# A retention and feed-forward kernel on one core: blocks of 256 tokens, nine equal tiles, 64-key chunks on quarters of the array

## The chip, the cores and the metric

The kernel runs on one core of one Trainium2 chip. The metric is device time in microseconds of one execution, and lower is better. One execution was also recorded by the hardware profiler; its times are counted from the first instruction of the program.

## What is computed

The reference joins two stages. The first is a retention layer on q, k and v, each of shape (8 batches, 8 heads, 576 positions, 64), the second a feed-forward layer with the activation h * cos(h) on 4608 tokens of width 512 and an inner width of 2048.

```python
scores = (q @ k^T) / sqrt(64)
gamma = 1 - 2 ** (-5 - head)
ret = scores * where(i >= j, gamma ** (i - j), 0)     # per head, i query, j key position
x = (ret @ v), heads side by side: (4608, 512)
h = x @ w_in                                           # (4608, 2048)
out = (h * cos(h)) @ w_out                             # (4608, 512)
```

Inputs and output are float32; the matmuls run in bfloat16.

## The kernel before

The decay factors as gamma ** i times gamma ** -j, so queries and keys are scaled by position tables first (`gq`, `gk`). Retention then needs no decay in the mask: within a group of tokens it is scores, a causal mask and a product with v; what came earlier enters through a running sum of k-times-v products per head, called the state. The positions are counted from the middle of a sequence, MID = 288.

Tokens are cut into 36 groups of 128. Sequences have 576 positions, so two sequences are nine groups, and in the group with index MIX = 4 of the nine the first half ends one sequence and the second half begins the next. For each group `load` fetches q, k and v with rows of 256 bytes, `prep` scales q and k on GpSimd into `qks` and rounds v to `vb`, and `transposes` makes `qkT`, on TensorE for the first six groups and by a transposing DMA afterwards. `scores` multiplies keys and queries into PSUM, and VectorE applies the mask into `ret`. `state` (for early groups) and `states` (for pairs of groups) form the k-times-v sums, `attn_out` adds the group's own product (`own`) and the product with the state (`carried`), and ScalarE copies the result to `xT`. Four groups at the very start share one load of q with 1024-byte rows (`fq4`).

The feed-forward part goes by tiles of tokens with widths 512, 256, 256 and seven times 512. `mm1` makes eight blocks of h per tile; for each, ScalarE takes the cosine into `cosh` and VectorE multiplies into `gT`. The blocks take turns on three PSUM areas, "a", "b" and "m". The second matmul has two forms. The first three tiles use `mm2`, sixteen products per 128 tokens. From the fourth tile on (S7 = 3), `mm2_seven` computes the 2x2 block product with seven products instead of eight, each of 16 matmuls of 256 columns, in the order 1, 2, 6, 4, 7, 5, 3. This needs sums of quarters of gT (`g_sum`, numbers 3, 5 and 6 on VectorE, number 7 on GpSimd) and of w_out (`w_sums`). PSUM areas "n" and "st" take the products' results.

The order of work on every engine is the order in which the Python code emits it (`manual_schedule`). Retention for later tiles is interleaved by hand: in the first three tiles through a list `todo` of positions in mm2's stream, later through the dictionary `at`, which calls `unit7` before product 2, 5, 6 or 3. `feed` paces loads, preparations and transposes by the stores of the output. Additions left over are kept in a list `pend` and emitted by `flush` at the next product.

Of the kernel before, what the change touches and what calls it, by code (L numbers as in the profile page):

```python
# [17 lines left out]
def kernel(  # L18
# [9 lines left out]

# [4 lines left out]
    HG = H // 2  # L39
    DM, DF = moe_w_in.shape  # L40
# [3 lines left out]
    NG = NTOK // P  # L44
    PER = 2 * S // P
    MIX = PER // 2
    HP = P // 2
# [3 lines left out]
    ET = DF // P  # L51

    widths = [512, 256, 256] + [512] * 7
    assert sum(widths) == NTOK
    starts = [sum(widths[:n]) for n in range(len(widths))]
    N_PE_T = 6
    S7 = 3
    LD = 5

    consts = ctx.enter_context(tc.tile_pool(name="consts", bufs=1))  # L60
    first = ctx.enter_context(tc.tile_pool(name="first", bufs=1))
    ld = ctx.enter_context(tc.tile_pool(name="ld", bufs=LD))
    nat = ctx.enter_context(tc.tile_pool(name="nat", bufs=8))
    trp = ctx.enter_context(tc.tile_pool(name="trp", bufs=8))
    retp = ctx.enter_context(tc.tile_pool(name="retp", bufs=4))
# [4 lines left out]
    op = ctx.enter_context(tc.tile_pool(name="op", bufs=2))  # L70
    xp = ctx.enter_context(tc.tile_pool(name="xp", bufs=2))

# [4 lines left out]

    pos_i = consts.tile([P, PER, H], I32)
    pos = consts.tile([P, PER, H], F32)
    lng = consts.tile([P, H], F32)  # L80
    gq = consts.tile([P, PER, H], F32)
    pos_i4 = consts.tile([P, 4, H], I32)
    pos4 = consts.tile([P, 4, H], F32)
    gq4 = consts.tile([P, 4, H], F32)
    gk = consts.tile([P, PER, H], F32)
    ln_scale = consts.tile([P, 1], F32)
    half_pi = consts.tile([P, 1], F32)
    tri = consts.tile([P, P], F32)
    tri_mix = consts.tile([P, P], F32)
    diag2 = consts.tile([P, P], F32)  # L90
    ident = consts.tile([P, P], BF16)
    zeros = consts.tile([P, 512], BF16)
    w_in_sb = consts.tile([P, DG, DF], BF16)
    w_out_sb = consts.tile([P, ET, DM], BF16)

    v_odd = consts.tile([P, 2, H, D], BF16)

    blocks4 = [consts.tile([P, HG, D], BF16, tag=f"sb{x}", name=f"sb{x}") for x in range(4)]

    tiles = {}  # L100
# [4 lines left out]
    def load(g, names="qkv", gate=None):  # L105

        t0 = g * P
        if g % PER == MIX:
            parts = [(0, HP, t0), (HP, P, t0 + HP)]
        else:  # L110
            parts = [(0, P, t0)]
        for name in names:
            src = {"q": q, "k": k, "v": v}[name]
            f = ld.tile([P, H, D], F32, tag="f" + name, name=f"f{name}")
            for p0, p1, t in parts:
                b, s0 = divmod(t, S)
                i = nc.sync.dma_start(
                    f[p0:p1], src[b, :, s0 : s0 + p1 - p0, :].rearrange("h s d -> s h d")
                )
                if gate is not None:  # L120
                    tc.add_manual_dep(
                        i.ins, gate.ins.name,
                        mybir.DependencyInfo(
                            mybir.DependencyClass.Sync, mybir.DependencyReason.DATA
                        ),
                        reason="weights first",
                    )
                    gate = None
            tiles["f" + name, g] = f

    def prep(g, early=False, kv_first=False):

        c = g % PER
        fk, fv = (tiles.pop(("f" + n, g)) for n in "kv")
        qks = nat.tile([P, 2, H, D], BF16, tag="qks", name="qks")
        vb = nat.tile([P, H, D], BF16, tag="vb", name="vb")
        qkT = trp.tile([P, 2 * HG, P], BF16, tag="qkT", name="qkT")

        def scaled(eng, m, f, by):
            eng.tensor_tensor(  # L140
                out=qks[:, m].rearrange("p (b a) d -> p a b d", a=2),
                in0=f.rearrange("p (a b) d -> p a b d", a=2),
                in1=by[:, c, :].rearrange("p (a b) -> p a b", a=2).unsqueeze(3).to_broadcast(
                    [P, 2, HG, D]
                ),
                op=ALU.mult,
            )

        if not early and not kv_first:
            scaled(nc.gpsimd, 0, tiles.pop(("fq", g)), gq)  # L150
        scaled(nc.vector if g == 3 else nc.gpsimd, 1, fk, gk)
        if early:
            tiles["fv", g] = fv
        else:
            nc.gpsimd.tensor_copy(vb, fv)  # L155
            if c == MIX and g > PER:
                nc.gpsimd.tensor_copy(v_odd[HP:, g // PER % 2], fv[HP:])
        if kv_first:
            scaled(nc.gpsimd, 0, tiles.pop(("fq", g)), gq)
        qT = qT4[:, :, g * P : (g + 1) * P] if early else qkT[:, :HG, :]  # L160
        tiles["a", g] = (qks, vb, qkT, qT)

    def transposes(g, banks=None, only=(0, 1)):
        qks, vb, qkT, qT = tiles["a", g]
        if g >= N_PE_T:
            nc.sync.dma_start(qkT, qks.rearrange("s m h d -> s (m h d)"), transpose=True)
            return
        for m in only:
            ps = psum.tile([P, HG, P], BF16, tag=banks[m], name="tr")
            for hg in range(HG):  # L170
                nc.tensor.transpose(
                    ps[:, hg, :],
                    qks[:, m, 2 * hg : 2 * hg + 2, :].rearrange("s h d -> s (h d)"),
                    ident,
                )
            nc.scalar.copy(qkT[:, m * HG : (m + 1) * HG, :], ps)
        if ("fv", g) in tiles and g != 3:
            nc.scalar.copy(vb, tiles.pop(("fv", g)))

    def warm(ps, n):  # L180


        for _ in range(n):
            nc.tensor.matmul(ps, lhsT=zeros[:, :P], rhs=zeros, start=True, stop=True)

    def scores(g, bank, idle=0, parts=1, put_off=None):
        qks, vb, qkT, qT = tiles["a", g]
        ps = psum.tile([P, 2, HG, P], F32, tag=bank, name="sc")
        warm(ps[:, 0].rearrange("p b i -> p (b i)"), idle)
        for hg in range(HG):  # L190
            for i0 in range(0, P, P // parts):
                for he in range(2):
                    d0, i1 = he * D, i0 + P // parts
                    nc.tensor.matmul(  # L194
                        ps[i0:i1, he, hg, :],
                        lhsT=qkT[d0 : d0 + D, HG + hg, i0:i1],
                        rhs=qT[d0 : d0 + D, hg, :],
                        start=True,
                        stop=True,
                    )  # L200
        ret = retp.tile([P, 2, HG, P], BF16, tag="ret", name="ret")
        mask = tri_mix if g % PER == MIX else tri
        tiles["ret", g] = ret

        def masked():
            nc.vector.tensor_tensor(  # L206
                out=ret.rearrange("p a b i -> p (a b) i"),
# [5 lines left out]
        if put_off is None:  # L213
            masked()
        else:
            put_off.append(masked)
# [502 lines left out]
    for g in (4, 5):  # L719
        prep(g)  # L720
# [148 lines left out]
```

## Time and profile before

| what | value |
|---|---|
| median of 3 runs | 301.75 us (301.12 to 301.95) |
| the profiled execution | 301.3 us |
| its span, first to last instruction | 299.6 us |
| TensorE busy | 286.9 us (96%) |
| VectorE busy | 215.1 us (72%) |
| ScalarE busy | 134.1 us (45%) |
| GpSimd busy | 138.9 us (46%) |
| granted TensorE clock, mean | 0.991 |
| DMA | 50.29 MB in 154305 packets |

Busy times are those of the profile's engine rows: PE is TensorE's matmuls, PEld its weight loads, DVE VectorE, ACT ScalarE, POOL GpSimd, SP the engine that issues most DMAs. Matmuls are pipelined, so their mean length holds some 0.2 us of latency; the distance between starts is what a matmul costs in a stream. A line such as `<-DVE gs L437` names what ended a wait: the VectorE instruction of line 437 that writes gs.

### The profile page before, as it was taken

The numbers are of one execution on the slowest core, as the hardware profiler recorded it, in microseconds if no ns is written. First come the engines' busy times: TensorE is split into PE (matmuls) and PEld (weight loads), VectorE is DVE, ScalarE is ACT, GpSimd is POOL, SyncE is SP. The second block draws the span as 40 slices with busy tenths as digits, with TensorE's granted clock in tenths as the row PEclk, the third lists the DMA queues.
The fourth block names the chain that finished last, engine by engine and source line by source line (L and its number), as shares of the span: only waits on it lengthen the run. The fifth ranks groups of instructions, "written<-read, shape, count | busy, mean of one in ns | idle before, by whom it ended". The sixth has DMA issues, their size and how long they took to land.

```text
span 299.6 us, 7314 instructions
## 1 busy us (share of the span) xinstructions
PE 286.9 (96%) x3105; PEld 196.5 (66%) x3105; DVE 215.1 (72%) x262; ACT 134.1 (45%) x163; POOL 138.9 (46%) x151
## 2 busy tenths in 40 slices
PE   7899999999999878999999999999999999999994
PEld 3478647848478757547854785488548854884584
DVE  6776717664568986599678966896689669925943
ACT  3556333515245314553355542644364445525620
POOL 2750067436345797473863791379238113101410
PEclk9999999999999979999999999999999999999998
DMA  8999999999999999997999999996960250011013
GB/s 210 214 210 207 209 217 194 218 210 237 202 170 227 209 242 222 201 233 165 213 216 247 199 218 206 194 234 160 209 117 3 79 135 0 31 51 63 0 37 106
DMA packets 154305, 50.29 MB, mean 168 GB/s; under 512 B 140832, under 2 KB 153248, under 8 KB 154272
## 3 DMA queue, kind: packets, MB, share of 16 engines
q1 hardware_dynamic: 149504, 45.10, 78.9%
q0 software_dynamic: 4224, 4.19, 8.4%
q8 instruction: 24, 0.39, 0.6%
q10 hardware_dynamic: 544, 0.52, 0.5%
q14 instruction: 9, 0.07, 0.1%
HBM read 36.70 MB, written 9.44 MB: 154 GB/s over the span
## 4 chain that ended last, share of the span: by engine, by line
PE 54%; DVE 5%; ACT 1%; issue 0%; DVEq 0%
PE h L364 25%; PE o L497 24%; DVE gT L373 2%; PE ov L332 1%; PE sc L194 1%; PE st L265 1%; PE ov L318 1%; DVE gs L437 1%; DVE ot L517 1%; DVE ret L206 1%; ACT cosh L372 0%; DVE s L286 0%; ACT ot L521 0%; DVEq L864 0%; DVEq L517 0%
## 5 line engine op out<-in xcount | busy, mean ns | idle before, releaser
L364 PE MATMUL h<-xT,w_in_sb 128*128 128x512 bf16 (+2 forms) x832 | 127.6, 314 | 0.8 <-DVE xT L349 0.7
L373 DVE TENSOR_TENSOR gT<-h,cosh 128x1024 bf16<-128x1024 f32 x72 | 88.0, 1223 | 37.3 <-ACT cosh L372 37.2
L372 ACT ACTIVATE cosh<-h,half_pi 128x1024 f32<-128x1024 f32 x72 | 80.2, 1114 | 66.7 <-PE h L364 66.0
L364 PEld LDWEIGHTS <-w_in_sb 128*128 128x128 bf16 x832 | 75.7, 98 | 50.0 <-issue 1.3
L437 POOL TENSOR_TENSOR gs<-gT 128x512 bf16<-128x512 bf16 x28 | 36.0, 1293 | 78.7 <-DVE gT L373 78.7
L140 POOL TENSOR_TENSOR qks<-fq,gq 128x512 bf16<-128x512 f32 x32 | 35.0, 1092 | 48.8 <-DMA fq<-in_q_dram 48.6
L497 PEld LDWEIGHTS <-gs 128*128 128x128 bf16 x456 | 44.0, 99 | 9.4 <-DVE gs L437 3.1
L140 POOL TENSOR_TENSOR qks<-fk,gk 128x512 bf16<-128x512 f32 x35 | 38.6, 1104 | 9.7 <-DMA fk<-in_k_dram 9.1
L206 DVE TENSOR_TENSOR ret<-sc,tri 128x1024 bf16<-128x1024 f32 x32 | 38.1, 1218 | 2.7 <-PE sc L194 2.7
L521 ACT COPY ot<-o 128x512 f32<-128x512 f32 x28 | 16.4, 586 | 45.7 <-PE o L497 44.6
L497 PEld LDWEIGHTS <-gT 128*128 128x128 bf16 x336 | 32.5, 98 | 6.0 <-DVE gT L373 0.6
L497 PE MATMUL o<-ws,gs 128*128 128x256 bf16 x224 | 28.4, 283 | 2.9 <-DVE gs L437 2.9
L517 DVE TENSOR_TENSOR ot<-ot,o 128x512 f32<-128x512 f32 x34 | 22.6, 682 | 11.0 <-ACT ot L521 7.9
L381 PE MATMUL o<-w_out_sb,gT 128*128 128x512 bf16 x128 | 30.1, 380 | 0.0
L497 PE MATMUL o<-w_out_sb,gs 128*128 128x256 bf16 (+1 forms) x232 | 26.8, 269 | 0.0
L497 PE MATMUL o<-w_out_sb,gT 128*128 128x256 bf16 x224 | 26.5, 273 | 0.3 <-DVE gT L373 0.3
L155 POOL CAST vb<-fv 128x512 bf16<-128x512 f32 x32 | 20.9, 652 | 8.3 <-DMA fv<-in_v_dram 7.7
L349 ACT CAST xT<-ov 128x1024 bf16<-128x1024 f32 (+1 forms) x18 | 16.5, 917 | 14.7 <-PE ov L318 12.6
L381 PEld LDWEIGHTS <-gT 128*128 128x128 bf16 x128 | 11.8, 98 | 12.5
L437 DVE TENSOR_TENSOR gs<-gT 128x512 bf16<-128x512 bf16 (+1 forms) x20 | 13.4, 672 | 0.3
L497 PE MATMUL o<-ws,gT 128*128 128x256 bf16 x112 | 13.4, 272 | 0.0
L391 ACT COPY ot<-o 128x512 f32<-128x512 f32 x8 | 4.7, 588 | 17.8 <-PE o L381 17.8
(69 smaller groups left out, 178.9 us busy)
## 6 DMA issues: line engine op xcount, KB each, us to landing
out_dram<-ot SPq DMA_DIRECT2D x35, 256.0 KB, 3.7
fk<-in_k_dram SPq DMA_DIRECT2D x32, 256.0 KB, 4.9
fv<-in_v_dram SPq DMA_DIRECT2D x32, 256.0 KB, 5.2
fq<-in_q_dram SPq DMA_DIRECT2D x30, 256.0 KB, 4.7
w_in_sb<-in_moe_w_in_dram POOLq DMA_DIRECT2D x4, 512.0 KB, 9.1
w_out_sb<-in_moe_w_out_dram POOLq DMA_DIRECT2D x4, 512.0 KB, 16.3
fq<-in_q_dram SPq DMA_DIRECT2D x8, 128.0 KB, 3.7
fk<-in_k_dram SPq DMA_DIRECT2D x8, 128.0 KB, 4.4
```

The lines of the kernel that those rows point to most:

```text
L140: eng.tensor_tensor(out=qks[:, m].rearrange("p (b a) d -> p a b d", a=2), in0=f.rearrange("p (a b) d -> p a b d", a=2), in1=by[:, c, :].re ...
L155: nc.gpsimd.tensor_copy(vb, fv)
L206: nc.vector.tensor_tensor(out=ret.rearrange("p a b i -> p (a b) i"), in0=ps.rearrange("p a b i -> p (a b) i"), in1=mask.unsqueeze(1).to_br ...
L349: evac(tiles["x", n][:, :, t0 : t0 + len(gs) * P], ps.rearrange("p c x i -> p c (x i)"))
L364: nc.tensor.matmul(ps[:, j, :], lhsT=w_in_sb[:, dg, (et + j) * P : (et + j + 1) * P], rhs=xT[:, dg, c0 : c0 + w], start=(dg == 0), stop=(d ...
L372: nc.scalar.activation(cosh, ps, ACTF.Sin, bias=half_pi, scale=1.0)
L373: nc.vector.tensor_mul(gT[:, et : et + m, c0 : c0 + w], ps, cosh)
L381: nc.tensor.matmul(ps, lhsT=gT[:, et, tsi * P : (tsi + 1) * P], rhs=w_out_sb[:, et, :], start=(et == 0), stop=(et == ET - 1),)
L437: eng.tensor_tensor(out=tiles["gs", n, x][:, e : e + step], in0=a[:, e : e + step], in1=b[:, e : e + step], op=op_,)
L497: nc.tensor.matmul(dst[i], lhsT=lhs[:, e, j * P : (j + 1) * P], rhs=rhs[:, e, c0:c1], start=(fresh and e == 0 and (i == 0 or len(parts) > 2)),
L517: return lambda: nc.vector.tensor_tensor(out=out_, in0=in0, in1=in1, op=ALU.add)
L521: nc.scalar.copy(t, tiles["all", x])
```

## The change

The kernel is written anew around the same two layers. Tokens are cut into 18 blocks of 256, two for each of nine tiles of 512. Tile 0 uses the plain second matmul, tiles 1 to 8 the seven products.

Queries of all blocks, and keys and values of the first six, are loaded with two neighbouring tokens in a partition (rows of 512 bytes); keys and values of later blocks keep one token a partition. Sub-block y of a block holds the even or odd tokens (or the first or second 128). A block's keys form chunks: two of 128 keys in blocks 0 to 5 (`pair`), four of 64 keys in blocks 6 to 17. Every chunk lies on one half of the partitions (x), so that with two heads (he) or two column halves four products of 64 rows and 64 columns lie on quarters of the array. Scores and carried products write PSUM in token order, that is with a stride of two. In `out_own` a drain of TensorE stands between the halves of the work. State sums are kept per chunk.

Blocks 0 to 3 are transposed on TensorE, later ones by DMA. Block 0 and 1 are worked through before mm1 starts, block 2 within tile 0's second matmul, block 3 in the middle of tile 1's mm1, and later ones between the seven products. Sum 7 is made on VectorE in tiles 1 and 2.

The core of the diff:

```diff
-    widths = [512, 256, 256] + [512] * 7
-    N_PE_T = 6
-    S7 = 3
-    LD = 5
+    W = 512
+    NT = NTOK // W
+    BK = 256
+    NB = NTOK // BK
+    NP_B = 6
+    AHEAD = 3
...
+    def scores(j, banks, idle=0):
...
+        for hg in range(HG):
+            for y in range(2):
+                for he in range(2):
+                    for x in range(2):
+                        c = cs[x] if pair else cs[2 * y + x]
+                        nc.tensor.matmul(
+                            in_order(pss[he][c.rows, hg, y, :]),
+                            lhsT=kT[he * D : he * D + D, 1, y, hg, c.rows],
+                            rhs=q_cols(c, he, hg),
+                            start=True,
+                            stop=True,
+                        )
...
+    def out_own(j, ps):
...
+        for swap in (1, 0):
+            for hg in range(0, HG, 2):
+                for c in cs:
+                    he = c.x ^ swap
+                    for y in c.subs:
+                        for h in (head(he, hg), head(he, hg + 1)):
+                            nc.tensor.matmul(
+                                ps[h % 2 * D : h % 2 * D + D, h // 2, c.c0 : c.c0 + c.n],
+                                lhsT=vb[c.rows, y, h, :],
+                                rhs=ret[c.rows, h // HG, h % HG, y, :],
...
+            if swap:
+                nc.tensor.drain()
...
-        eng, step = (nc.gpsimd, 2) if x == 7 else (nc.vector, e1 - e0)
+        eng, step = (nc.gpsimd, 2) if x == 7 and n > 2 else (nc.vector, e1 - e0)
...
+        if n == 1:
+            slots = {0: "w04", 1: "w48", 5: ((7, 0, E2),), 6: ((5, 0, 4),)}
...
             if x == 6:
-                late_sums(n, (3,))
+                late_sums(n, (3, 7) if n < 3 else (3,))
...
+    load(0, "kqv")
+    load(1, "kqv")
...
+    round_v(0)
+    more_tables()
+    scaled(nc.gpsimd, 1, "k", 0)
+    scaled(nc.gpsimd, 1, "k", 1)
+    w_dma = [load_w_in(e, e + 512) for e in range(0, DF, 512)]
+    m0 = scores(0, "ab", idle=2)
+    m0[0]()
+    transpose_pe(1, "k", 0, "n", act)
+    add0 = sums_of(0, "st")
+    m0[1]()
+    add0()(act)
+    scaled(nc.gpsimd, 1, "q", 0)
+    scaled(nc.vector, 1, "q", 1)
+    more_tables2()
+    out_own(0, ps0)
+    out_carried(0, ps0)
...
+    transpose_pe(1, "q", 0, "n", act)
+    transpose_pe(1, "q", 1, "st", act)
+    m1 = scores(1, "ab", idle=2)
+    m1[0]()
+    round_v(1)
+    add1 = sums_of(1, "st")
+    m1[1]()
+    add1()(act)
+    w_dma += [load_w_out(e, e + 4) for e in range(0, ET, 4)]
+    load_next(names="kq", gate=w_dma[5])
...
+    def intro(j, sc_banks, st_bank, put_off=None):
+        ms = scores(j, sc_banks)
+        add = sums_of(j, st_bank)
+        run = [*ms, lambda: add()()]
+        if put_off is None:
+            for f in run:
+                f()
+        else:
+            run[0]()
+            put_off += run[1:]
...
+            if n == 0 and i == 0:
+                inside = {2: lambda: outputs(1, "m", act, vec)}
...
+                if i == 3:
+                    early(3, "q")
+                    steps_to(5)
+                if i == 4:
+                    intro(3, "ab", "st")
+                    outputs(3, "m", act, vec)
+            mm1(n, et, c0, cw, {0: "abmabmab", 1: "abmmabma"}.get(n, "abmabmab")[i], inside)
...
+            todo += [(34, lambda: intro(2, "ab", "b")), (52, lambda: outputs(2, "a", act, vec))]
...
+        def only_intro(flush, pend):
+            flush()
+            intro(a, sc_banks(a), "m" if a < NP_B else "b", pend)
+
+        def mid_unit(flush, pend):
+            flush()
+            outputs(a, "m")
+            intro(b, sc_banks(b), "st" if b < NP_B else "b", pend)
...
+        if n in (1, 2):
+            at = {6: only_intro, 5: mid_unit, 3: end_unit}
+        elif n < last:
+            at = {2: first_unit, 5: second_unit}
```

`sums_of` makes the chunks' k-times-v products into one PSUM area and returns the addition to the running state, one addition for both chunks in blocks 0 to 5 and one for each chunk later. `outputs` calls `out_own`, `out_carried` and the copy to `xT`. `early` prepares or transposes blocks 2 and 3; `steps_to` prepares later blocks on GpSimd, two tiles ahead. `first_unit` and `second_unit` call `outputs` for a block and `intro` for the next; in tile n, a is block 2n + 2 and b is block 2n + 3. In the preamble, `more_tables` holds nine iotas and the masks on GpSimd, `more_tables2` the position tables on VectorE and ScalarE.

## The prediction

> **What bounds the kernel now.** I read the page, then windows cut at the tiles of 512 rows, then the timeline around the one early hole, then single groups for durations.
>
> ```profile
> PE 286.9 (96%) x3105; PEld 196.5 (66%) x3105; DVE 215.1 (72%) x262; ACT 134.1 (45%) x163; POOL 138.9 (46%) x151
> PE 54%; DVE 5%; ACT 1%; issue 0%; DVEq 0%
> ```
>
> TensorE is nearly always busy, so its stream plus its holes is the time. The windows (columns: length, then busy of PE, PEld, DVE, ACT, POOL with instructions, then granted clock) show where the holes are: the fifth window, the first tile with the seven products (mm2_seven), against a steady tile.
>
> ```profile
> 0.00:19.30 19.30, 16.43 (x170) 9.13 (x171) 13.67 (x32) 9.81 (x16) 11.31 (x24) 1.00 1.11 213
> 84.20:120.90 36.70, 33.01 (x450) 28.00 (x449) 28.50 (x31) 15.99 (x20) 26.13 (x26) 0.95 1.25 215
> 181.90:211.20 29.30, 29.30 (x323) 19.66 (x322) 23.43 (x28) 14.20 (x17) 16.98 (x17) 1.00 1.02 189
> ```
>
> The timeline names the hole: TensorE waits 2.9 us for a VectorE sum, and after it the clock is halved for 3 us.
>
> ```profile
> 103.19 0.64 PE L194 MATMUL sc<-qkT 64*64 64x128 bf16 x32
> 104.62 2.05 DVE L437 TENSOR_TENSOR gs<-gs,gT 128x2048 bf16<-128x2048 bf16 x1
> 106.73 3.50 PE L497 MATMUL o<-ws,gs 128*128 128x256 bf16 x16 [2.90 <-DVE gs L437]
> ```
>
> ```profile
> 107.00:110.00 3.00, 3.00 (x16) 2.13 (x15) 3.00 (x4) 0.00 (x0) 3.00 (x4) 0.50 1.24 267
> ```
>
> A steady tile is 13.8 (mm1, 64 matmuls of 512 columns at 216 ns) + 12.25 (112 of 256 columns at 109 ns) + 2 x 1.62 (the retention of 256 tokens: state sums, own, carried, scores) = 29.3, with no wait. So a change that only trims VectorE or DMA there gains nothing; one that adds waits in the early tiles pays in full.
>
> **Costs of the pieces.** Lines that carry the prices:
>
> ```profile
> L206 DVE TENSOR_TENSOR ret<-sc,tri 128x1024 bf16<-128x1024 f32 x32 | 38.1, 1218 | 2.7 <-PE sc L194 2.7
> L373 DVE TENSOR_TENSOR gT<-h,cosh 128x1024 bf16<-128x1024 f32 x72 | 88.0, 1223 | 37.3 <-ACT cosh L372 37.2
> L140 POOL TENSOR_TENSOR qks<-fk,gk 128x512 bf16<-128x512 f32 x35 | 38.6, 1104 | 9.7 <-DMA fk<-in_k_dram 9.1
> ```
>
> The groups give means in ns after the bar; the timeline gives start and length in us:
>
> ```profile
> 198.26 0.42 PE L318 MATMUL ov<-qkT,sb 64*64 64x128 bf16 x16
> 236.35 0.37 PE L318 MATMUL ov<-qkT,sb 64*64 64x128 bf16 x16
> 236.55 0.62 PE L194 MATMUL sc<-qkT 64*64 64x128 bf16 x32
> 5.84 1.05 PE L688 MATMUL tr<-ident,qs 128*128 128x128 bf16 x8
> 8.50 0.40 PE L171 MATMUL tr<-ident,qks 128*128 128x128 bf16 x4
> ```
>
> *Retention on quarters.* Scores already run on quarters: 32 products of 128 columns in 0.62, of which 0.2 is the last one's latency, so 56 ns for four. The carried line at 236.35 holds eight products of 64 columns and is 0.05 shorter than its full twin at 198.26: a wave of four at 64 columns takes 28 ns. A block of 256 tokens in 64-key chunks has 32 products each of scores, sums, own and carried: 4 x 8 waves x 28 ns = 0.9, plus a drain between own's halves (0.2, by the 0.15 between the last own and first carried start, a change of array shape) and two shape changes (0.2): 1.3. Scores and carried now write PSUM with stride 2. L688 writes with stride 4 and needs 109 ns where L171 needs 55; stride 2 is not in the trace, so between 0 and +0.45 a block; I take +0.2, nearer L688. So 1.5 against 1.62, ends 1.3 and 1.75: twelve blocks give -1.5 (-4 to +1.5). Their VectorE work: one mask of 1.22 instead of two, but up to four adds of 0.42 instead of two; no gain on the path.
> The Trainium skill ("TensorE: Matmul & The Clock Gate", section "Wait — 56ns, not 53.3ns?") says starts never come closer than about 25 ns however few the columns, which speaks against cutting products in two. By it a block is 128 x 25 ns = 3.2 (estimate) and the whole 20 us slower than my sum; the line at 236.55 shows 32 products in 0.62 us, and the measurement decides.
> Blocks 0 to 5 keep 128-key chunks: 2.15 each (scores 0.45, sums 0.5, own 0.65, carried 0.25, changes 0.3); blocks 2 and 3 add 16 transposes on TensorE, 1.05.
>
> *One more tile by seven products.* 13.8 becomes 12.25: -1.55.
>
> *The start.* Loads of 512-byte rows land in order k0, q0, v0, k1, q1, v1. In before a 1024-byte packet takes 46 ns, a 256-byte one 18, the few of 512 bytes 27: 1024 of these on 16 engines are 1.75, so landings come at about 4.9, 6.6, 8.3, 10.1, 11.8, 13.5 (before's 1 MB of q landed at 6.05, packets and 1.2 us more). GpSimd then works in order: round v0 (2 x 0.65) to 9.6, more_tables (nine iotas of 0.2, masks, copies, memsets: 3.3) to 12.9, k1 (2 x 1.1) to 15.1, four w_in issues (0.82 each) to 18.4, half of q1 to 19.5. From there nothing hides: transposes and copies 1.6, scores 0.9, two masks 2.45, sum 0.7, rounding 0.6, carried 0.45 give 26.3 before mm1 runs on. In before the same point (8 of mm1's matmuls done, tile 0's rows ready) is 19.3: +7.0. TensorE has no work from 9.7 to about 14 and again around 17 to 19; a hole of 2.9 halved the clock above, so mm1 starts at half: +2.0 (0 to 3.5).
>
> *Tile 0.* mm1 13.1, mm2 13.8, block 2 3.2. The sums of block 2 take bank "b", which its second mask still reads: TensorE stands while VectorE does two masks, +2.55. Loads of block 2, gated behind w_out, land by 43, needed from 46: hidden by 3 us; if the weights came 3 us later it would show. Tile 0 ends at 26.3 + 2.0 + 32.65 = 61.0.
>
> *Tile 1 is where it is decided.* Each engine keeps the order in which the kernel writes its work, so what stands behind a waiting product waits too. From the tile's start: block i=3 of mm1 uses bank "m" right after i=2 did, so it waits for cosine (1.12) and gT (1.22): 2.1 lost; i=3 ends at 10.15. Then scores and sums of block 3 (1.0), and outputs(3) at once behind them, with the rest of mm1 queued after. Outputs(3) need gT(3) (VectorE to 12.7), two masks (15.15), the add (15.85), its rounding (16.5), carried and the copy to x: i=4 starts at 17.85, 7.7 after i=3's end for 2.0 of work. The hole halves the clock: +1.7. mm1 ends at 26.5. From 24.4 VectorE is the bound, without a gap. What its sums cost depends on GpSimd: 1024 elements took 1.45 at 100.46 beside a GpSimd sum and 0.69 at 191.42 without one.
>
> ```profile
> 100.46 1.45 DVE L437 TENSOR_TENSOR gs<-gT 128x1024 bf16<-128x1024 bf16 x1
> 191.42 0.69 DVE L437 TENSOR_TENSOR gs<-gT 128x1024 bf16<-128x1024 bf16 x1
> ```
>
> GpSimd should be idle by then (blocks 5 to 7 prepared by about 20 into the tile, block 8's loads not yet issued), so I take 0.7 for 1024 and 1.4 for 2048; the page's mean of these rows would add 3. The run: gT(5) 1.23, sum 7 1.4 (on VectorE here, not GpSimd), gT(6) 1.23, half of 5 0.7, gT(7) 1.23, half of 5 0.7, sum 6 1.4, add 0.7, mask 1.22, sum 3 1.4, sum 7 a second time (the code asks for it twice) 1.4, mask 1.22, add 0.7: 14.5, to 38.9. Outputs(4) wait for that; scores(5) end at 40.6; product 5 shares bank "st" with block 5's sums and waits for both masks and the add, to 44.0; product 5, outputs(5) and product 3 end at 48.5. Pure TensorE work in it is 33.9 (14.0 + 12.25 + 1.2 of transposes + 3 x 2.15): 14.6 of waits. Before's comparable tile lost 2.9 + 0.8 + 1.7 of clock.
>
> *Tile 2* has the same late sums on VectorE (gT(7) 3.1 behind mm1's end, then the sums): product 6 +0.3, product 7 +0.7, carried(7) +1.0; 26.1 + 3 x 1.5 + 2.0 = 32.6.
>
> *Tiles 3 to 7*: 26.1 + 2 x 1.5 = 29.1 each, the last without an intro (-0.6). GpSimd has 16.6 per tile there (eight scalings of 1.1, two casts of 1.3, four sums of 1.29), DMA about 21 of 29: neither ends last. *Tile 8*: 26.1; *tail* 4.0 as in before (span 299.6, TensorE's end 295.6).
>
> **Sum.** 61.0 + 48.5 + 32.6 + 144.9 + 26.1 + 4.0 = 317.1 of span. Before's span is 299.6 in an execution of 301.3, 1.7 around it, and the median shown is 301.75, 0.15% above the profiled one. So 318.8, rounded to 319.
>
> **Rivals.**
> - *No waits (not slower).* One mechanism: VectorE's queue in tile 1. If its run from gT(5) to the add of block 4 took under 10 us instead of 14.5, and the masks did not stand between scores and outputs, TensorE would be the bound in tiles 0 to 2: -2.55 - 14.6 - 2.0, so 299.7. For it: before's tile 84.2:120.9 has 28.5 of VectorE work and loses only 5. Against: there the masks are asked for long before their use, here in the same breath, and every duration above is a measured row. Chance 0.08.
> - *Half the waits.* GpSimd's tables take less and the start costs +4; tile 1 loses 7.3, not 14.6: 319 - 3 - 7.3 = 308.5. For: iotas of small shapes may cost less than the rows I used (0.13 for 64x8), and landings are estimates. Chance 0.16.
> - *Quarters do not pay and the clock stays low.* Stride 2 costs as stride 4 (+0.25 a block of twelve, +0.7 in blocks 2 to 5: +6) and tiles 1 and 2 run at half clock after each of three more holes (+1.7 each): 330. Chance 0.14.
> - *It doesn't do what it says*: products on quarters go one at a time, 28 ns each: 128 x 28 ns = 3.6 a block, +25: 344. The 0.62 us line speaks against it. Chance 0.02.
>
> **How the numbers follow.** The forecast keeps 0.60. Its own ends: start 24.5 to 28, clock 0 to 3.5 and 0 to 3 in the two holes, chunks -2.4 to +3, VectorE sums up to +3: about 311 to 330. With the half-waits case the range is 305 to 330; outside lie the no-waits case and half of the slow one. Under 0.3% (0.9 us) nothing can be told from no change here. Faster 0.08 is the no-waits case, same 0.02 is taken from the edge of the half-waits case, slower 0.90 is the rest.
>
> **What would show it.** First full run of mm1 near 26 (not 19); a hole of 2.5 in tile 0's mm2 ended by the mask; in tile 1 a hole near 4 us before own of block 3, ended by VectorE, and waits for gs and for bank "st" by product 5; granted clock below 0.97. Steady tiles 28.7 to 29.6: above 30 the strides cost more, below 28.5 the quarters paid. Wrong would be: tile 1 under 40 us, or TensorE's first hole gone before 20 us.

## The result and the profile after

The changed kernel takes 331.5 us (331.3 to 332.5), the kernel before 301.4 us in the same comparison: a ratio of 1.101 (95% interval 1.097 to 1.105). The median of 332.0 on record counts a fourth execution, of 1664 us, which is left aside here. The direction was forecast, the size was not: +30.1 us against +17.3, and the time lies 1.5 us above the range.

The head of the page, then its chain of waits and its DMA line. The profiled execution took 331.5 us, 1.7 around its span as before.

```profile
span 329.8 us, 8764 instructions
PE 296.4 (90%) x3824; PEld 204.0 (62%) x3842; DVE 220.2 (67%) x279; ACT 141.9 (43%) x164; POOL 140.3 (43%) x156
PE 62%; DVE 15%; DMA 9%; POOL 5%; issue 4%; ACT 2%; SPq 1%; DVEq 0%; ACTq 0%; POOLq 0%
DMA packets 124199, 49.86 MB, mean 151 GB/s; under 512 B 80512, under 2 KB 123648, under 8 KB 124160
```

TensorE is busy for 9.5 us more and idle for 20.7 us more (33.4 against 12.7 of the span). Part of the added busy time is matmuls at half clock, of which more below. The larger rows did cut the packets, from 154305 to 124199; no run tells what that alone bought. In the chain of waits VectorE now holds 15%, where it held 5%, and DMA 9%, where before's chain had none.

The windows of the changed kernel (columns as before): retention ahead of mm1, tile 1 in four parts, and a steady tile.

```profile
15.00:25.20 10.20, 8.08 (x143) 5.79 (x144) 4.66 (x8) 4.04 (x9) 9.11 (x12) 0.50 0.90 142
...
62.70:73.40 10.70, 8.18 (x85) 7.15 (x87) 8.74 (x10) 5.98 (x9) 9.21 (x10) 1.00 1.01 244
73.40:80.50 7.10, 3.12 (x114) 2.46 (x114) 4.12 (x5) 2.32 (x3) 3.95 (x4) 0.95 1.33 188
80.50:90.60 10.10, 9.96 (x64) 7.52 (x64) 3.90 (x4) 3.35 (x3) 5.08 (x5) 0.69 0.72 127
90.60:113.60 23.00, 19.50 (x314) 15.85 (x313) 15.69 (x18) 6.30 (x9) 5.08 (x5) 0.93 0.75 156
...
210.00:240.20 30.20, 29.63 (x417) 20.08 (x417) 23.00 (x30) 14.98 (x17) 16.18 (x14) 1.00 0.72 150
```

Tile 1, 62.7 to 113.6, takes 51.0 us: TensorE's busy times in its four rows add to 40.8, so 10.1 are idle, and the clock is low in parts of its second half. Of the 7.1 us from 73.4 TensorE works 3.1. The answer on TensorE's waits (total us, times, longest) names first the start's waits for keys and queries (the longer one ends at 14.85), then the holes that the prediction walked through, in tile 1 (own of block 3, mm1's block 3, product 5) and in tile 0 (block 2's sums):

```profile
PE tr L214 <- POOL qks L171: 5.6, 2, 4.6
PE ov L380 <- DVE ret L265: 3.1, 1, 3.1
PE h L436 <- DVE gT L445: 2.5, 1, 2.5
PE st L305 <- DVE ret L265: 2.5, 1, 2.5
PE o L540 <- DVE s L339: 2.4, 1, 2.4
...
PE o L540 <- ACT ot L562: 1.6, 3, 1.1
```

The last line was not in the forecast. Nor was a pause of 1.8 us in tile 2, inside own of block 7, for which the profile shows nothing that TensorE waited for; its cause is open. The retention of one block in tile 3, from the timeline (start, length, engine, line):

```profile
163.94 0.74 PE L380 MATMUL ov<-ret,vb 64*64 64x64 bf16 x32
164.50 0.62 PE L398 MATMUL ov<-qkT,sb 64*64 64x64 bf16 x32
164.92 0.65 PE L254 MATMUL sc<-qkT 64*64 64x64 bf16 x32
165.37 0.45 PE L305 MATMUL st<-vb,qks 64*64 64x64 bf16 x32
```

Four kinds of 32 products with 64 columns. Own and the state sums write PSUM in one piece, carried and scores with stride 2. The state sums take 0.45 and the scores 0.65, each with about 0.2 of latency in it: by the single starts in the trace a wave of four products takes 32 ns with unit stride and 56 ns with stride 2. Between own's halves the drain leaves 0.29 without a start. From own to the next product (165.75) it is 1.8 us (1.7 in other blocks), before had 1.62, the forecast 1.5.

### The profile page after: what moved, and what is told of

Read it like the earlier page. It is cut to its first block, busy times and chain, and to the rows that moved or that the text cites. A ratio compares the mean times of both kernels' runs of the same rounds, so it can differ in the third digit from the quotient of the medians.

```text
span 329.8 us, 8764 instructions
## 1 busy us (share of the span) xinstructions
PE 296.4 (90%) x3824; PEld 204.0 (62%) x3842; DVE 220.2 (67%) x279; ACT 141.9 (43%) x164; POOL 140.3 (43%) x156
## 2 busy tenths in 40 slices
DMA packets 124199, 49.86 MB, mean 151 GB/s; under 512 B 80512, under 2 KB 123648, under 8 KB 124160
## 4 chain that ended last, share of the span: by engine, by line
PE 62%; DVE 15%; DMA 9%; POOL 5%; issue 4%; ACT 2%; SPq 1%; DVEq 0%; ACTq 0%; POOLq 0%
PE h L436 29%; PE o L540 23%; DMA w_out_sb<-in_moe_w_out_dram 5%; DVE gT L445 4%; DMA fv<-in_v_dram 4%; DVE gs L483 3%; PE ov L380 3%; PE ov L398 2%; DVE ret L265 2%; PE sc L254 2%; DVE ot L558 1%; SPq L140 1%; PE o L847 1%; PE st L305 1%; POOL vb L183 1%
## 5 line engine op out<-in xcount | busy, mean ns | idle before, releaser
L436 PE MATMUL h<-xT,w_in_sb 128*128 128x512 bf16 (+1 forms) x690 | 129.2, 345 | 4.8 <-DVE gT L445 2.5
L171 POOL TENSOR_TENSOR qks<-fq,gq 128x512 bf16<-128x512 f32 x33 | 36.7, 1132 | 37.2 <-DMA fq<-in_q_dram 26.2
L360 ACT CAST sb<-s 128x768 bf16<-128x768 f32 (+3 forms) x18 | 14.8, 820 | 58.9 <-DVE s L350 30.4
L562 ACT COPY ot<-o 128x512 f32<-128x512 f32 x32 | 18.2, 585 | 26.3 <-PE o L540 26.0
L171 POOL TENSOR_TENSOR qks<-fk,gkc 128x512 bf16<-128x512 f32 x24 | 27.3, 1155 | 0.1
L380 PE MATMUL ov<-ret,vb 64*64 64x64 bf16 (+1 forms) x576 | 13.6, 212 | 6.9 <-DVE ret L265 3.1
L483 DVE TENSOR_TENSOR gs<-gT 128x512 bf16<-128x512 bf16 (+2 forms) x26 | 19.0, 730 | 0.6
L171 POOL TENSOR_TENSOR qks<-fk,gkp 128x512 bf16<-128x512 f32 x10 | 11.1, 1124 | 19.2 <-DMA fk<-in_k_dram 19.2
L421 ACT CAST xT<-ov 128x1024 bf16<-128x1024 f32 x14 | 14.2, 1012 | 10.8 <-PE ov L398 10.7
L380 PEld LDWEIGHTS <-vb 64*64 64x64 bf16 x576 | 8.9, 110 | 13.1 <-issue 12.9
L350 DVE TENSOR_TENSOR s<-st,s 128x256 f32<-128x256 f32 x37 | 15.6, 422 | 0.9
L282 DVE TENSOR_TENSOR ret<-sc,mask_c 128x1024 bf16<-128x1024 f32 x12 | 14.6, 1218 | 2.1 <-PE sc L254 2.1
```

The lines of the kernel that those rows point to most:

```text
L171: return eng.tensor_tensor(out=dst.rearrange("p b a d -> p a b d"), in0=src.rearrange("p (a b) d -> p a b d", a=2), in1=by.rearrange("p (a ...
L282: nc.vector.tensor_tensor(out=ret.rearrange("p a b r i -> p (a b r) i"), in0=both.rearrange("p a b r i -> p (a b r) i"), in1=mask_c.unsque ...
L350: nc.vector.tensor_tensor(out=s32[:, u], in0=at(c), in1=s32[:, u - 1] if u else tiles["run"], op=ALU.add,)
L360: run(sb, s32)
L380: nc.tensor.matmul(ps[h % 2 * D : h % 2 * D + D, h // 2, c.c0 : c.c0 + c.n], lhsT=vb[c.rows, y, h, :], rhs=ret[c.rows, h // HG, h % HG, y, :],
L436: nc.tensor.matmul(ps[:, j, :], lhsT=w_in_sb[:, dg, (et + j) * P : (et + j + 1) * P], rhs=xT[:, dg, c0 : c0 + w], start=(dg == 0), stop=(d ...
```

## The experiments

All were timed beside the kernel before, whose median was 300.6 to 301.5 in these comparisons. Only e2, e6 and e12 came out at the time that their theory had named, the last two at the upper end of it; the others gained less, except e9, which gained more. Tile lengths are those of each run's profile, from the first matmul of a tile's mm1 to that of the next, and stand where the text reads them.

| run | us | ratio to before (95%) | tile 0 | tile 1 | tile 2 | steady |
|---|---|---|---|---|---|---|
| the change | 331.5 | 1.101 (1.097 to 1.105) | 36.7 | 51.0 | 34.6 | 30.2 |
| e1_unit_stride | 328.7 | 1.090 (1.087 to 1.094) | 38.9 | 49.7 | 34.5 | 29.9 |
| e2_round_late | 328.5 | 1.092 (1.088 to 1.095) | 38.0 | 51.0 | 33.6 | 29.8 |
| e5_unit_and_round | 325.8 | 1.081 (1.073 to 1.090) | 39.1 | 48.3 | 35.1 | 29.2 |
| e3_start_order | 332.1 | 1.099 (1.094 to 1.104) | 45.0 | 48.6 | 34.8 | 30.2 |
| e7_start_and_gate | 328.4 | 1.091 (1.084 to 1.099) | 43.2 | 48.2 | | |
| e4_tile1_early | 332.4 | 1.103 (1.099 to 1.106) | | 50.8 | | |
| e6_tile1_banks | 328.6 | 1.090 (1.083 to 1.096) | | 45.2 | | |
| e9_four_wide_blocks | 326.0 | 1.083 (1.078 to 1.088) | 38.4 | 46.2 | 32.6 | 30.2 |
| e10_plain_tile1 | 327.8 | 1.090 (1.085 to 1.094) | | 47.3 | 33.7 | |
| e8_all_seven | 315.2 | 1.045 (1.040 to 1.049) | 41.1 | 43.2 | 33.6 | 29.2 |
| e11_all_plain_tile1 | 310.8 | 1.033 (1.029 to 1.036) | 36.6 | 41.3 | 34.8 | 29.2 |
| e12_sum7_on_gpsimd | 307.1 | 1.020 (1.016 to 1.025) | 37.2 | 40.6 | 31.5 | 29.2 |

**The steady tile: stride and rounding.** e1 lets TensorE write even and odd tokens one after the other and puts them in order in the copy to x.

```diff
     def in_order(ap):
-        return ap.rearrange("p (i r) -> p r i", r=2)
+        return ap.rearrange("p (r i) -> p r i", r=2)
...
+    def moved(run, j, x, ps, d0, d1):
+        k = len(chunks[j])
+        run(
+            x[:, d0:d1].rearrange("p c (k i r) -> p (c k) r i", k=k, r=2),
+            ps[:, d0:d1].rearrange("p c (k r i) -> p (c k) r i", k=k, r=2),
+        )
...
```

> Edit: scores and carried products are written to PSUM in the order even tokens, odd tokens (unit stride) instead of token order (stride 2); the masks are built in that order, and the copy to x puts the tokens back. Theory (the stride-2 write doubles the price): in the changed kernel a wave of four products of 64 columns starts 56 ns after the one before in scores and carried, against 32 ns in own and in the state sums. With unit stride all are near 30: 16 waves x 25 ns = 0.4 us per block, 0.8 per steady tile (30.2 to 29.4), and with blocks 0 to 5 (0.4 to 0.6 each, part of it under VectorE waits) 5 to 8 us in all: 324 to 327 us. Rival A (the 56 ns come from reading the queries in two pieces, or from the weight loads): nothing moves, 332. Rival B (the copy to x, now with a scattered output, becomes slow): ScalarE's copy rises from 1.0 to 2 us and eats some or all of it, 328 to 333.

The waves of scores and carried fell to 32 to 34 ns, but the tile gained only 0.3. The same block of e1 in the timeline, with the copy to x and a wait ahead of a later product:

```profile
164.48 0.43 PE L398 MATMUL ov<-qkT,sb 64*64 64x64 bf16 x32
164.73 0.47 PE L254 MATMUL sc<-qkT 64*64 64x64 bf16 x32
165.00 1.31 ACT L417 CAST xT<-ov 128x1024 bf16<-128x1024 f32 x1 [0.39 <-PE ov L398]
172.20 1.91 PE L547 MATMUL o<-w_out_sb,gs 128*128 128x256 bf16 x16 [1.30 <-ACT ot L569]
```

The products' lengths fell by 0.2 each and the copy, now reordering, grew from 1.01 to 1.31 us. From own to the next product a block takes 1.44 to 1.53 us in e1 and e5, 1.70 to 1.82 in the change: the stride costs 0.26 to 0.29 a block. So the two blocks of a steady tile became 0.54 shorter, and 0.28 of it went into the wait for ScalarE ahead of product 7, which grew from 0.26 to 0.54. That wait comes from ScalarE's queue, shown here for the changed kernel, tile 3:

```profile
169.27 1.34 DVE L350 TENSOR_TENSOR s<-st,s 128x256 f32<-128x256 f32 x3
170.65 1.05 ACT L360 CAST sb<-s 128x1024 bf16<-128x1024 f32 x1 [4.46 <-DVE s L350]
171.60 1.07 ACT L562 COPY ot<-o 128x512 f32<-128x512 f32 x2
172.23 1.91 PE L540 MATMUL o<-w_out_sb,gs 128*128 128x256 bf16 x16 [1.06 <-ACT ot L562]
```

ScalarE stands 4.5 us idle at the rounding of the state, which waits for a copy and three adds on VectorE. Two product copies are queued behind it. The first is of product 6, whose last matmul ended at 169.4, so it could have run some 2 us earlier (in e2 it starts at 169.76), and product 7 needs the area that it frees. e2 emits the rounding behind the copies.

```diff
-        run = [*ms, lambda: add()()]
+        run = [*ms, lambda: add()() if put_off is None else rounds.append(add())]
...
             elif x == 6:
                 u1 = copied("b", 1)
+                round_now()
             elif x == 4:
                 c21 = copied("c", 4)
+                round_now()
...
```

> Edit: the rounding of a block's state sums on ScalarE is put behind the copies of products 6 and 4 instead of ahead of them. Theory (a ScalarE queue wait): in tiles 3 to 6 TensorE stands 1.06, 0.69, 0.26 and 0.26 us ahead of product 7, because product 7 needs the copy of product 6's area, and that copy stands behind the rounding, which waits for VectorE's four adds. With the order turned round these gaps vanish: -2.3 us in tiles 3 to 6, with up to 1 more in tiles 1 and 2: 329 us. Rival (the gap is VectorE's own lateness or the bank's): the gaps stay and the time is 332; or outputs of the next block wait for the later rounding and it is 332 to 333.

> Edit: unit-stride writes and the late rounding together. With unit stride alone the steady tile fell only from 30.2 to 29.9, although 0.8 us of waves went: the wait ahead of product 7 grew from 0.26 to 0.54 us, because what TensorE saves is waited for at ScalarE's queue. Theory (two limits in a row): with both edits the waits are gone and the steady tile is 30.2 - 0.77 - 0.26 = 29.2 or less; the whole gains more than the sum of the two (3.3 + 3.5 us): 324 to 325 us. Rival (the edits gain by the same thing, or the copy to x at 1.3 us is a new limit): steady tile 29.5 or more and 326 to 329 us.

Alone the rounding takes 0.4 from a steady tile; with both edits (e5) it is 29.2, 1.0 less, and tiles 3 to 7 together are 146.9 where the change had 151.4. So the two causes are shown, and in the steady tile each hid part of the other: 0.3 and 0.4 alone, 1.0 together. Off the median the edits took 2.8 and 3.0 us alone and 5.7 together; what of it lies in the early tiles is not told apart, since their half-clock stretches moved too (mean clock 0.947 in e1 and e5, 0.963 in the change).

**The start.** e3 lets GpSimd prepare block 1's queries and values ahead of the tables.

```diff
     round_v(0)
-    more_tables()
     scaled(nc.gpsimd, 1, "k", 0)
...
+    scaled(nc.gpsimd, 1, "q", 0)
+    round_v(1)
...
+    more_tables()
```

> Edit: in the preamble GpSimd scales keys and queries of block 1 and rounds its values before it issues the w_in loads and makes the tables of later blocks; the VectorE and ScalarE part of those tables comes after block 1's sums. Theory (GpSimd's queue sets the start): block 1's second half of q is scaled at about 13 instead of 19 us, so mm1 first runs on at 21 to 23 instead of 28.7: -5 to -7 us, limited by the first w_in part, which is issued near 14.5 and lands near 20.5: 325 to 327 us. Rival (loads set the start: v of block 1 lands last): TensorE's first mm1 moves by under 2 us and the time is 330 or more.

mm1 runs on 5.6 us earlier (23.1 instead of 28.7), and the end does not move. GpSimd's and TensorE's lines of the timeline of e3 around block 2:

```profile
43.10 2.04 POOL L171 TENSOR_TENSOR qks<-fk,gkp 128x512 bf16<-128x512 f32 x2 [17.95 <-DMA fk<-in_k_dram]
44.20 0.61 PE L214 MATMUL tr<-ident,qks 128*128 128x128 bf16 x4 [3.58 <-POOL qks L171]
```

This is the cover that the prediction named, block 2's loads behind the weights, and here it runs out: they land at 43 as forecast, TensorE comes for them earlier, waits 3.6 and then runs 6.9 us (43.5 to 50.4) at a granted clock of 0.51. e7 moves the weight loads and the gates of block 2 forward too.

```diff
...
-    load_next(names="kq", gate=w_dma[5])
-    load(2, "v", gate=w_dma[6])
+    load_next(names="kq", gate=w_dma[3])
+    load(2, "v", gate=w_dma[5])
```

> Edit: the start's order as before, the first two w_in parts issued ahead of block 1's value rounding, and block 2's loads of k and q gated by the last w_in part instead of the second w_out part (its v by the second w_out part). In the run with the old gate mm1 ran on 5.6 us earlier, but TensorE then stood 3.6 us in tile 0's second matmul for block 2's keys, which landed at 43.1, and lost the clock. Theory (the gate was the cover that ran out): mm1 runs on at 22, block 2's keys land by 33, no wait at the transposes, and the gain of the start is kept: 324 to 326.5 us. Rival (the weights then come late, as both share the DMA engines): TensorE waits for w_out in the second matmul, and 328 to 332 us.

mm1's first matmul comes 6.9 us earlier than in the change (19.1) and tile 1 only 0.4 earlier (62.3): waits of 1.44 and 0.60 for the same block and two stretches of 3.4 us at half clock give most of it back. Of the 3.6 us that its span is shorter, most stands in tile 1 (48.2).

**Tile 1.** e4 moves block 3's scores one place forward in mm1, so that its masks are done long before its own product.

```diff
                 if i == 0:
                     early(3, "prep")
+                if i == 1:
+                    early(3, "k")
                 if i == 2:
-                    early(3, "k")
+                    early(3, "q")
                 if i == 3:
-                    early(3, "q")
                     steps_to(5)
+                    intro(3, "ab", "st")
                 if i == 4:
-                    intro(3, "ab", "st")
                     outputs(3, "m", act, vec)
```

> Edit: in tile 1 the transposes, scores, masks and sums of block 3 come one mm1 block earlier, so that one mm1 block lies between them and outputs(3). Theory (TensorE stands because outputs follow their masks at once): in the changed kernel i=3 of mm1 ends at 73.3 and i=4 starts at 80.5 with 3 us of work between; the holes of 2.5 (bank m) and 3.1 + 0.7 shrink together by 3 to 4 us, and the halved clock behind them may go too (0 to 1.7): 326.5 to 329. Rival (tile 1 is bound by VectorE's total): what is won at outputs(3) is lost again before product 6 or product 5, and the time stays within 1 us of 332.

```profile
73.91 2.34 DVE L265 TENSOR_TENSOR ret<-sc,mask_p 128x1024 bf16<-128x1024 f32 x2
78.55 1.22 DVE L445 TENSOR_TENSOR gT<-h,cosh 128x1024 bf16<-128x1024 f32 x1 [1.70 <-ACT cosh L444]
79.82 0.95 PE L380 MATMUL ov<-ret,vb 64*64 64x128 bf16 x32 [3.87 <-DVE gT L445]
```

The masks are done at 76.25 and own still starts at 79.82, behind gT of mm1's block 3, since outputs(3) share the area "m" with that block. Two conditions held the place, and lifting the first alone gave nothing; the second alone was not tried. e6 is e4 with the areas in plain turn.

```diff
-            mm1(n, et, c0, cw, {0: "abmabmab", 1: "abmmabma"}.get(n, "abmabmab")[i], inside)
+            mm1(n, et, c0, cw, "abmabmab"[i], inside)
```

> Edit: block 3 in tile 1 one mm1 block earlier as before, and mm1's blocks take areas a, b, m in turn, so that i=3 uses a and outputs(3) finds m free. In the run without this, outputs(3) began 0.05 us after gT of i=3, which held area m, and nothing was won. Theory (area m was the second limit): outputs(3) begins when the masks are done; i=4 starts 14 us into the tile instead of 17.8, and tile 1 is 4 to 5 us shorter (51 to 46.5): 327 to 328.5 us. Rival (VectorE's total binds tile 1): i=4 is earlier but products 6, 7 and 5 wait that much longer, and the time is 331 or more.

Tile 1 falls from 51.0 to 45.2; its holes of 2.5 and 3.1 are replaced by one of 1.69 for the masks, and no stretch of it runs at half clock. mm1's block i=4 starts 14.65 us into the tile instead of 17.80, so the order of the areas and the masks asked for at the last moment cost 3.2 us there. The rest is clock: the end of mm1 is 2.0 shorter and product 5 is 1.5 shorter, more than the 2.6 that are left, so other places lost a little. The hole of 2.42 ahead of product 5 is still there. The median fell by 3.0 only; in the profiled execution tile 0 was 1.7 longer, with a stretch at half clock that the change does not have there.

**Fewer 128-key blocks.** e9 sets `NP_B = 4`, so blocks 4 and 5, which tile 1 works through, have 64-key chunks and one mask.

> Edit to the changed kernel: only blocks 0 to 3 have 128-key chunks; blocks 4 and 5 have 64-key chunks too, so one mask of 1.22 us instead of two, and their state sums go to area b instead of st. Theory (the wait of product 5 for area st, 2.4 us, and the masks bind the end of tile 1): tile 1 is 2.4 to 4.5 us shorter than the profiled 51.0: 327.5 to 329.5 us. Rival (VectorE's adds of 0.42 for each chunk, up to four instead of one of 0.68, give it back, or the sums now wait for area b): within 1 us of 332.

5.5 us, more than expected: tile 1 46.2, tile 2 32.6, and no half clock after 85.2, where the change has 1.5 us more of that stretch and two further ones of 3.4. In tile 1 the wait of 2.4 ahead of product 5 is gone, and with it 1.6 of half clock. Tile 2 works on blocks of 64-key chunks in both kernels, so its 2.1 are not a mask's: its half clock and the pause of 1.8 inside own are absent, and a wait of 1.3 has come. e10 then gives tile 1 the sixteen products of tile 0 and needs no sums of gT there.

```diff
...
-            if n:
+            if n > 1:
                 sums_after(n, i)
-        if n == 0:
+        if n < 2:
             gT = tiles["g", n]
...
```

> Edit to the run with four wide blocks: tile 1 makes its second matmul by sixteen products for each 128 tokens, as tile 0 does, with the retention of blocks 4 and 5 between them; sum 7 of w_out is made in tile 2. TensorE's work rises by 1.55 us; VectorE loses sums of 7 us and adds of 4 us in tile 1. Theory (in tile 1 VectorE is the bound, so seven products cost there instead of saving): tile 1 falls to 42 to 44 us (14.0 + 13.8 + three blocks at 2.1 to 3 + 1.2 of transposes + 7.5 of waits at block 3), 5 to 7 us less, and the time is 321 to 325. Rival (TensorE is what counts and the sums only fill its waits): the time rises by 1 to 2 us over the run with four wide blocks.

It is 1.7 us slower than e9. VectorE's late run is gone, but the waits ahead of block 3 (2.0 and 3.1) stand, one of 1.2 us for gT is new ahead of scores, and TensorE's products are 1.55 us more. The rival of this run came true: with the other holes still there VectorE's run alone did not set tile 1's length.

**All together.** e8 joins e5, e6, e7 and e9 with two more edits: sum 7 of tile 1 is asked for once, and tile 0's scores, sums and outputs stand apart.

```diff
-                late_sums(n, (3, 7) if n < 3 else (3,))
+                late_sums(n, (3, 7) if n == 2 else (3,))
...
-            todo += [(34, lambda: intro(2, "ab", "b")), (52, lambda: outputs(2, "a", act, vec))]
+            todo += [
+                (34, lambda: [m() for m in scores(2, "ab")]),
+                (46, lambda: sums_of(2, "b")()()),
+                (60, lambda: outputs(2, "a", act, vec)),
+            ]
```

> Edit: unit stride, late rounding, the start with the new gate, block 3 early with areas in turn, and three more: in tile 0 the state sums of block 2 stand 12 matmuls behind its masks (2.5 us of wait in the changed kernel) and its outputs 8 later; sum 7 of tile 1 is made once, not twice (1.2 us of VectorE); 128-key chunks end with block 3 instead of 5, so that the sums of block 5 use area b and product 5 doesn't wait for area st (2.4 us). Theory (waits of the early tiles and the stride are all of the loss): 332 - 7.5 - 4.5 - 6.5 - 2.5 - 1.2 - 2.4 = 307.5, and 1 to 4 less for halved clock: 304 to 308 us. Rival (each gap closed opens the next one, as in two runs so far): 312 to 320 us.

> Edit to the run with all seven edits (315.2): tile 1 by sixteen products as well; the sums of w_out move from tile 0 to tile 1, and block 2's outputs come 6 matmuls earlier, since TensorE waited 2.6 us there for VectorE's copy to x behind those sums. Theory: tile 1 from 43.2 to 36 to 38, tile 0 shorter by 2 to 3, tile 2 longer by up to 1: 305 to 309 us. Rival (the saved VectorE time isn't the bound any more after the other edits): 313 or more.

> Edit to the run before: sum 7 of tile 2 is made on GpSimd in four parts during mm1, as in later tiles and in the kernel before, not on VectorE behind mm1. Theory (VectorE's late sums hold up tile 2): its 33.6 us fall by 1.2 to 3, the holes of 1.7 and 1.3 us ahead of product 7 and of the carried products shrink: 303 to 307 us. Rival (GpSimd is busy with the preparation of blocks 8 to 11, and product 7 waits for it): no gain or 1 to 2 us more.

e8 reaches 315.2, 16.3 us below the change; e5, e6, e7 and e9 alone add to 17.2, so they add up nearly, and the two further edits show no gain. The time lies in the range of its rival; but as the edits add up, most of what the theory counted too high had been missing in the single runs already. Two of its largest waits of TensorE are new, for VectorE's copy to x (3.9 us in three) and for the rounding (2.8 in three); the wait for GpSimd's scaling is 3.5, where the change had 5.6.

e11 adds e10's tile 1 to it and moves the sums of w_out out of tile 0: 4.3 us less, which is short of its theory, most of it in tile 0 (4.4; tile 1 gains 1.9, tile 2 loses 1.2). Part of the 4.4 is clock: e8's tile 0 has a stretch at half clock (41.5 to 45.0), e11's none. e12 gives tile 2's sum 7 back to GpSimd, which loads VectorE no longer there: tile 2 falls from 34.8 to 31.5, and 307.1 is the best version, still 2.0% slower than the kernel before. Its steady tile, 29.2, ties with before's 29.3. The first 1024 tokens end at 96.1, before at 84.2: 11.9 us lost. The 512 tokens behind them take 31.5 where before's first tile with seven products took 36.7, the rest is 2.3 us shorter, and the span ends 4.4 us later.

One more variant, scores between own's halves in place of the drain, was not tried. What the drain alone costs at the end is open.

## Why the prediction was right and wrong

The span was forecast at 317.1 and is 329.8. By stage, measured against forecast:

| stage | forecast | measured | miss |
|---|---|---|---|
| start to the end of tile 0's mm1 | 41.4 | 42.2 | +0.8 |
| rest of tile 0 | 19.6 | 20.5 | +0.9 |
| tile 1 | 48.5 | 51.0 | +2.5 |
| tile 2 | 32.6 | 34.6 | +2.0 |
| tiles 3 to 7 | 144.9 | 151.4 | +6.5 |
| tile 8 and tail | 30.1 | 30.2 | +0.1 |

**Right: the direction, and the mechanism of the first 1024 tokens.** Tile 0's hole of 2.55 (2.52), tile 1's walk up to i=4 at 17.85 from its start (17.80), GpSimd idle so that the sums of 2048 ran near their short price (1.2 us), and product 5 behind area "st" (2.4) all came as written. e6, e9 and e12 moved or removed the masks, the areas' order and a VectorE sum, and the tiles became shorter: these are causes, not only neighbours of the holes. "VectorE is the bound" in tile 1 is too strong: e10 took its late run away and gained nothing.

**Luck: the size of the start's miss, and tile 0's clock.** mm1 runs on at 28.7, not 26.3. It was to begin at half clock, which was priced at 2.0; instead the retention ahead of it ran at half clock (15.0 to 25.2) and mm1 at full (granted clock 1.00 from 25.2 to 42.2). A term too short and one that did not come leave +0.8. Tile 0's hole was followed by full clock; in e1 to e7, e9 and e10, which have it too, 3.4 us at half clock followed.

**Wrong: the price of a block.** Of the term 1.5 three parts were too small. The wave was put at 28 ns and is 32, the drain at 0.2 and is 0.29: without the stride the block was forecast at 1.3 and takes 1.44 to 1.53 (e1, e5). The stride, "I take +0.2, nearer L688", costs 0.26 to 0.29; +0.2 is in fact nearer nothing than L688's 0.45. The trace had the right row: stride 4 doubled L171's 55 ns to 109 ns, and stride 2 gave 56 ns for 32, nearly the same factor. The Trainium skill ("SBUF — State Buffer", section "Door 1: The DMA port swizzle") says that PSUM has lines of 8 bytes, two float32 values, and that any access to it that isn't contiguous slows matmuls significantly. The runs agree, and it is the rule that spoke against this change most directly. A block of 64-key chunks costs 1.7 to 1.8 instead of 1.5, some 0.5 us in each steady tile.

In blocks of 128-key chunks the stride was left out altogether: 2.15 has scores at 0.45 without a word on it. The scores of block 4, in the change and in e1:

```profile
94.21 1.07 PE L254 MATMUL sc<-qkT 64*64 64x128 bf16 x32
94.21 0.64 PE L254 MATMUL sc<-qkT 64*64 64x128 bf16 x32
```

Up to the next product it is 0.86 against 0.48. Such a block takes about 3 us, and the difference is about tile 0's miss. In tile 1 most of it fell into waits that were there anyway: up to product 5 the tile was within 0.5 us of the forecast.

**Wrong: "Tiles 3 to 7: neither ends last".** GpSimd and DMA were weighed there, ScalarE was not: its queue was put at nothing without a reason. It was busy 14.2 of 29.3 us in before, but it works in order: the rounding, moved ahead of two copies by the new order, made 0.26 us of wait in a steady tile and 1.06 in tile 3. e2 removed it, and with e1 the steady tile is what the forecast said (29.2 against 29.1). Of the miss of 6.5 both edits took back 4.5; the rest is mostly tile 4 (30.6 in e5), where TensorE pauses 1.2 us inside a product (0.85 in the change) and the profile shows nothing that it waited for. That cause is open.

**Wrong in size: half clock in the early tiles.** The forecast had two low stretches costing 3.7 us, 1.7 of it in tile 1. The change has 23.9 us at half clock before its end (15.0 to 25.2, 79.9 to 86.7, and 3.4 each from 107.2 and 144.7), against one stretch of 3.4 in before. One of them begins at the product behind the hole for area "st":

```profile
106.98 3.45 PE L540 MATMUL o<-ws,gs 128*128 128x256 bf16 x16 [2.42 <-DVE s L339]
```

An estimate of the price, by the matmuls that became longer: the last 64 of tile 1's mm1 take 10.1 us and 64 x 109 ns are 7.0; this product takes 3.4 and a product at full clock 1.8; the last product of tile 2 takes 3.2. That is about 6 us in tiles 1 and 2, for four times 3.4 us at half clock, where 1.7 for one was forecast. It is the largest part of the misses of these two tiles; tile 2 has the pause of 1.8 inside own besides.

**The rivals.** "No waits" and "half the waits" are refuted by tile 1's 10.1 us of idle time. "Quarters go one at a time" is refuted by 32 products in 0.45 us. The rival at 330 came near: its three more stretches at half clock came, and so did a stride that costs more in the blocks of 128-key chunks. But the stride of the other blocks was far below its price, +0.25 a block over the sum (0.06 to 0.09), and the queue of ScalarE is not in it, so its number is in part luck.

## What to carry to other kernels

Price a PSUM write with a stride as a doubled product until a row shows less, don't interpolate toward nothing, and put the term into every product that has one. For every engine that frees a buffer, read its queue in the order of emission and not its busy share: one instruction that waits there holds all that are ready behind it. A gap closed in an early stage can be taken back by the next gate, shared area or clock stretch (5.6 us earlier in e3 gave nothing, and e4 gave nothing until e6 moved the area too), so look for the second condition before the edit.

## What the runs showed of the hardware

- Four products on quarters of the array start 3 to 9 ns apart, and a wave of four takes 32 ns at 64 columns; with a stride of 2 in PSUM it is 56 ns. At 128 columns the two are 56 and 108 ns.
- A drain of TensorE between dependent halves left 0.29 us without a start.
- The clock does not fall by the length of a hole alone. In the change the hole of 2.52 us at tile 0's sums left the clock at 1.00; in e7 the same hole, also 2.52, was followed by 3.4 us at half. And the hole of 2.42 ahead of product 5 was followed by half clock in the change, not in e6.

In all profiles of this case the low stretches are 1 to 5 times 3.41 us long, and within a profile they begin and end on one grid of 3.41 us. So the busy share of TensorE was read by the windows of that grid. The hole in the change (51.61 to 54.13) is split over two windows, of which the emptier one is the first line; in e7 it lies in one, the second line, and the third line follows it (the first number behind the length is TensorE's busy time):

```profile
52.54:55.95 3.41, 1.66 (x36) 1.16 (x38) 2.50 (x4) 0.24 (x1) 3.41 (x5) 1.00 1.21 222
49.77:53.18 3.41, 1.10 (x34) 0.87 (x35) 2.50 (x3) 0.00 (x0) 3.33 (x5) 1.00 1.22 215
53.20:56.60 3.40, 3.40 (x10) 1.21 (x8) 3.28 (x4) 0.62 (x1) 3.40 (x4) 0.50 1.22 221
```

TensorE is busy for 49% of the first window and for 32% of the second. Over the 14 profiles every window at full clock that was under 43% busy was followed by half clock, and none that was over 60%; between them both occur, and these runs don't say what decides there. The Trainium skill ("TensorE: Matmul & The Clock Gate", section "What's actually happening") describes a window of about 3.4 us that runs free of the instructions, and idle windows that halve the clock. The lengths and the grid agree with that; that a window only partly idle is enough, and that the same hole costs or not by where it falls on the grid, is what these runs add.
